# Idle matmuls ahead of the first output tile: float32 zeros in place of bf16 zeros

## The chip, the cores and the metric

The kernel runs on one core of one Trainium2 chip. The metric is the device time of one execution in microseconds, the median of several runs. One more execution was recorded by the hardware profiler; its rows are what the text reads.

## The reference, cut to what matters

A two-step attention (landmarks `p` attend to `k` and `v`; the queries attend to the result) is followed by a feed-forward layer with a quadratic gate:

```python
def _attn_ref(q, k, v, p):                      # 8 batches, 8 heads, 576 tokens, 64 wide, 32 landmarks
    p_packed = sm_attn(p, k, v)
    out = sm_attn(q, p_packed, p_packed)
    return out.astype(np.float32)

def _moe_ref(x, w_in, w_out):                   # x: 4608 x 512, w_in: 512 x 2048, w_out: 2048 x 512
    h = x @ w_in
    g = np.where(h >= 1, h, np.where(h <= -1, 0.0, (h + 1) ** 2 / 4.0))
    return (g @ w_out).astype(np.float32)
```

Nothing of the change takes part in this: the idle matmuls multiply zeros, and what they write is never read.

## The kernel before, in words

For each of the 8 batches the kernel turns `k` and `q` so that the head dimension lies across the partitions (for the first two batches by transposes on TensorE, line 564 and line 601), forms the landmark scores (line 667), exponentiates them (line 676), packs the values with them (lines 735 and 740, "the packed matmul"), and forms the second scores (line 770), their exponentials (line 828) and their sums (line 835). The rows of `w_in` are multiplied with the packed values (line 792, tile `mp`, copied to `M` by line 333), the normalised weights `A` are made by VectorE (line 851), and `M` with `A` gives the hidden tile `h` (line 939). ScalarE and VectorE apply the gate (lines 945 to 960) and leave `hT`; 16 matmuls of 512 columns with `w_out` give an output tile of 128 tokens (line 1030), which is copied and stored. All matmuls take bf16 operands and accumulate in float32.

The order of the work on every engine is written out ahead. `Plan.run` (line 55) simulates the kernel in Python with fixed costs for each step and gives a sorted list; lines 1110 to 1113 emit it in that order, so the program of each engine is fixed, and at run time an instruction waits only for its data and buffers.

The idle matmuls are put in afterwards. Lines 1095 to 1103 walk over the planned steps of TensorE up to the first output matmul and note every planned pause as a number `n` of units: up to 5 us of planned time one unit stands for 0.2135 us, after that for 0.1085 us, with 0.1 us left free. `warm(n)` (line 1105) takes an output tile in PSUM and fills the pause with matmuls of 128 x 128 zeros by 512 columns of zeros, each worth two units, and one of 256 columns where `n` is odd. The operands come from one tile, `zeros` (line 361), which VectorE clears once at the start (line 367). Nobody waits for the idle matmuls, but TensorE works off its instructions in order, so the real matmul behind a burst starts after it.

Of the kernel before, what the change touches and what calls it, by code (L numbers as in the profile page):

```python
# [130 lines left out]
def kernel(  # L131
# [11 lines left out]
    f32 = mybir.dt.float32  # L143
    bf16 = mybir.dt.bfloat16
# [7 lines left out]
    P = 128  # L152
# [9 lines left out]
    FW = 512  # L162
# [150 lines left out]
    const = ctx.enter_context(tc.tile_pool(name="const", bufs=1))  # L313
# [44 lines left out]
    ones2 = const.tile([P, 2, 2], bf16)  # L358
    kz = const.tile([P, H, C5, D], bf16, name="kz")
    vz = const.tile([P, C5, H, D], bf16, name="vz")  # L360
    zeros = const.tile([P, FW], bf16)
    pT_all = const.tile([P, B * Q * G * X * NP + X * NP], bf16, name="pT")
    pT = pT_all[:, :B * Q * G * X * NP].rearrange("p (b a g x n) -> p b a g x n", b=B, a=Q, g=G, x=X)
    hT = const.tile([P, KF, 2 * S], bf16)
# [732 lines left out]
    for t in (t for t in order if t.engine == "PE"):  # L1097
        if t.start >= first_o:
            break
        n = math.ceil((t.start - at) / 0.2135) if at < 5.0 else int((t.start - at - 0.1) / 0.1085)  # L1100
# [3 lines left out]

    def warm(n):
        o = psO.tile([P, d_model], f32, tag="o", name="o")
        for w in [FW] * (n // 2) + [FW // 2] * (n % 2):
            nc.tensor.matmul(o[:, :w], zeros[:, :P], zeros[:, :w], start=True, stop=True)  # L1108

    for t in order:  # L1110
        while fill and t.start > fill[0][0] and t is not consts:
            warm(fill.pop(0)[1])
        t.ways[t.engine][2](t.engine)
# [30 lines left out]
```

## Time and profile before

| | |
|---|---|
| median of 3 runs | 241.79 us (241.51 to 241.95) |
| the profiled execution | 242.18 us |
| its span, first to last instruction | 240.4 us |
| TensorE busy in the span | 233.2 us (97%), 2096 matmuls |
| ScalarE, VectorE, GpSimd busy | 190.0, 179.4 and 37.7 us |
| mean granted clock of TensorE | 0.998 |

In the rows, PE is TensorE's matmul, PEld its weight load, DVE is VectorE, ACT ScalarE, POOL GpSimd; "o<-zeros" names the tile written and the tiles read. Recorded durations of matmuls include the way through the array, so matmuls that follow each other at 0.216 us are shown as lasting 0.379 us each; what a stream of them costs is read from the distance of their starts, or from the chain.

### The profile page before, as it was taken

The page shows a single profiled execution, that of the slowest core. Times are in us where ns is not written, and L with a number is a line of the kernel's source. Part 1 is how long each engine was busy: PE and PEld are TensorE (multiplying, and loading weights), DVE is VectorE, ACT ScalarE, POOL GpSimd, SP SyncE. Part 2 cuts the span into 40 slices and gives each one's busy share as a digit, 9 for nine tenths or more (in the row PEclk, how much of TensorE's full clock was granted, in tenths as well). Part 3 has the DMA queues.
Part 4 walks back from the last instruction along what each step waited for, and adds up shares of the span by engine and source line. Part 5 has one row for each costly group of instructions (what it writes and reads, how often), then busy time and mean ns, then how long its engine had stood idle before and what let it go on. Part 6 is the DMA issues. An engine that isn't in the chain of part 4 may idle for free.

```text
span 240.4 us, 5315 instructions
## 1 busy us (share of the span) xinstructions
PE 233.2 (97%) x2096; PEld 133.9 (56%) x2096; DVE 179.4 (75%) x320; ACT 190.0 (79%) x324; POOL 37.7 (16%) x57
## 2 busy tenths in 40 slices
PE   7799999999999999999999999999999999999993
PEld 3555565565555655466546655656456554654452
DVE  4549997499977996699868989999469967995000
ACT  3578898799989986899889898998789886984211
POOL 8552306000510040070005000300000000000000
PEclk9999999999999999999999999999999999999999
DMA  7999999999999999999999997989301210111315
GB/s 155 201 206 207 203 202 206 199 257 171 148 188 248 186 171 204 187 174 213 204 183 197 218 213 117 138 189 203 97 2 48 74 33 27 44 40 52 98 45 119
DMA packets 65353, 36.42 MB, mean 152 GB/s; under 512 B 34480, under 2 KB 60848, under 8 KB 65328
## 3 DMA queue, kind: packets, MB, share of 16 engines
q0 software_dynamic: 28080, 18.26, 53.5%
q1 hardware_dynamic: 36544, 17.28, 33.4%
q10 hardware_dynamic: 704, 0.56, 0.8%
q8 instruction: 16, 0.26, 0.4%
q14 instruction: 9, 0.07, 0.1%
HBM read 37.22 MB, written 9.44 MB: 194 GB/s over the span
## 4 chain that ended last, share of the span: by engine, by line
PE 92%; ACT 3%; DMA 2%; DVE 1%; issue 0%
PE o L1030 51%; PE h L939 26%; PE mp L792 3%; DMA k_raw<-in_k_dram 2%; PE o L1108 2%; PE pk L730 2%; PE sm L835 2%; PE sp L652 2%; PE s L770 1%; PE tp L564 1%; ACT M L333 1%; PE pk L740 1%; DVE M L333 0%; ACT rc L846 0%; PE tp L601 0%; PE sp L667 0%
## 5 line engine op out<-in xcount | busy, mean ns | idle before, releaser
L1030 PE MATMUL o<-w_out_sb,hT 128*128 128x512 bf16 (+1 forms) x592 | 146.3, 374 | 0.0
L960 DVE SCALAR_TENSOR_TENSOR hT<-t 128x576 bf16<-128x576 f32 (+1 forms) x130 | 91.9, 742 | 3.7 <-ACT t L955 2.1
L945 ACT ACTIVATE x<-h 128x576 f32<-128x576 f32 (+1 forms) x130 | 79.2, 646 | 11.6 <-PE h L939 10.7
L1030 PEld LDWEIGHTS <-hT 128*128 128x128 bf16 x592 | 55.3, 98 | 49.3 <-issue 5.6
L939 PE MATMUL h<-A,M 128*128 128x288 bf16 x512 | 78.1, 286 | 0.6 <-ACT M L333 0.4
L939 PEld LDWEIGHTS <-M 128*128 128x128 bf16 x512 | 49.6, 98 | 27.7 <-issue 1.5
L953 DVE TENSOR_SCALAR t<-x 128x576 f32<-128x576 f32 (+1 forms) x75 | 33.6, 463 | 10.6 <-ACT x L945 10.2
L955 ACT ACTIVATE t<-x 128x576 f32<-128x576 f32 (+1 forms) x55 | 37.0, 684 | 0.9
L333 ACT COPY ob<-o 128x512 f32<-128x512 f32 (+1 forms) x21 | 11.9, 567 | 16.5 <-PE o L1030 16.3
L851 DVE SCALAR_TENSOR_TENSOR A<-eT,rs,rc 128x576 bf16<-128x576 bf16 (+1 forms) x18 | 12.9, 747 | 10.7 <-ACT rc L846 10.7
L333 ACT CAST M<-mp 128x1024 bf16<-128x1024 f32 (+1 forms) x19 | 17.7, 969 | 2.5 <-PE mp L792 2.4
L430 POOL DMA_DIRECT2D v<-in_v_dram x14 | 10.2, 731 | 52.2 <-DVE vz L708 48.9
L430 POOL DMA_DIRECT2D kz<-in_k_dram x14 | 9.7, 701 | 50.9 <-DMA kT<-kz 50.2
L333 DVE CAST M<-mp 128x1024 bf16<-128x1024 f32 (+1 forms) x15 | 17.2, 1147 | 0.4 <-PE mp L792 0.4
L333 DVE COPY ob<-o 128x512 f32<-128x512 f32 x16 | 10.9, 685 | 2.7 <-PE o L1030 2.6
L1108 PE MATMUL o<-zeros 128*128 128x512 bf16 (+1 forms) x42 | 11.4, 405 | 1.2 <-DVE zeros L367 1.2
L828 ACT ACTIVATE eT<-s,rs 128x576 bf16<-128x576 f32 x16 | 11.1, 736 | 1.8 <-PE s L770 1.2
L841 ACT ACTIVATE ln<-sm 128x576 f32<-128x576 f32 x16 | 10.1, 651 | 1.9 <-PE sm L835 1.7
L846 ACT ACTIVATE rc<-ln 128x576 f32<-128x576 f32 (+1 forms) x18 | 10.6, 634 | 0.0
L792 PE MATMUL mp<-w_in_sb,ppT 64*32 64x512 bf16 x256 | 10.3, 380 | 0.0
L674 ACT ACTIVATE ex<-sp 128x640 bf16<-128x640 f32 x14 | 9.5, 702 | 0.3 <-PE sp L652 0.2
L444 POOL DMA_DIRECT2D q<-in_q_dram x11 | 8.4, 762 | 5.1 <-ACT x L945 2.1
(62 smaller groups left out, 110.7 us busy)
## 6 DMA issues: line engine op xcount, KB each, us to landing
out_dram<-ob SPq DMA_DIRECT2D x23, 192.0 KB, 2.7
q<-in_q_dram POOLq DMA_DIRECT2D x7, 576.0 KB, 16.1
out_dram<-ob SPq DMA_DIRECT2D x24, 128.0 KB, 3.9
kz<-in_k_dram POOLq DMA_DIRECT2D x7, 320.0 KB, 6.4
v<-in_v_dram POOLq DMA_DIRECT2D x7, 320.0 KB, 8.6
w_out_sb<-in_moe_w_out_dram POOLq DMA_DIRECT2D x4, 512.0 KB, 15.3
kz<-in_k_dram POOLq DMA_DIRECT2D x7, 256.0 KB, 7.3
v<-in_v_dram POOLq DMA_DIRECT2D x7, 256.0 KB, 9.6
```

Of the source, the lines that this page charges most:

```text
L333: i = (nc.vector.tensor_copy if e == "DVE" else nc.scalar.copy)(to, of)
L430: return G_.dma_start(tokens(nm, b)[p0:p0 + R5, :, :c * D], of)
L792: i = nc.tensor.matmul(have["mp", b, f][a * NP:(a + 1) * NP, g], have["ppT", b][r, g, a], w_in_sb[r, a, f * FW:(f + 1) * FW], start=True, ...
L828: nc.scalar.activation(have["eT", b, g][:, part], have["s2", b, g][:, part, :HALF], AF.Exp, scale=rs_of[b][:, g, 1:])
L851: V.scalar_tensor_tensor(have["A", b][:, g, part], have["eT", b, g][:, part], rs_of[b][:, g, :1], have["rc", b, g][:, part], ALU.mult, ALU ...
L939: nc.tensor.matmul(have["h", b, fi][:, hf, :HALF], have["M", b][:, g, fi * P:(fi + 1) * P], have["A", b][:, g, hf], start=(g == 0), stop=( ...
L945: nc.scalar.activation(have["x", b, fi][:, hs[0]:hs[-1] + 1], have["h", b, fi][:, hs[0]:hs[-1] + 1, :HALF], AF.Prelu, bias=-1.0, alpha=0.5)
L953: V.tensor_scalar(t, x, 1.0, 0.0, ALU.add, ALU.max)
L955: nc.scalar.activation(t, x, AF.Relu, bias=1.0)
L960: V.scalar_tensor_tensor(dst, t, 1.0, t, ALU.min, ALU.mult)
L1030: m = nc.tensor.matmul(have["o", key][:, :w], hT[:, fi, i * P:(i + 1) * P], w_out_sb[:, fi, cols], start=(fi == 0), stop=(fi == KF - 1))
L1108: nc.tensor.matmul(o[:, :w], zeros[:, :P], zeros[:, :w], start=True, stop=True)
```

## The change

The tile of zeros gets half as many elements of twice the width, and `warm` fills a pause with matmuls of 256 float32 columns, one for four units, and one of 64, 128 or 192 columns for a rest of one, two or three units.

```diff
-    zeros = const.tile([P, FW], bf16)
+    zeros = const.tile([P, FW // 2], f32)
...
     def warm(n):
         o = psO.tile([P, d_model], f32, tag="o", name="o")
-        for w in [FW] * (n // 2) + [FW // 2] * (n % 2):
+        for w in [FW // 2] * (n // 4) + [FW // 8 * (n % 4)] * (n % 4 > 0):
             nc.tensor.matmul(o[:, :w], zeros[:, :P], zeros[:, :w], start=True, stop=True)
```

## Rows read from the trace of the kernel before

**Rows 1.** Page: busy us, share, instructions; granted clock in 40 slices.

```profile
PE 233.2 (97%) x2096; PEld 133.9 (56%) x2096; DVE 179.4 (75%) x320; ACT 190.0 (79%) x324; POOL 37.7 (16%) x57
...
PEclk9999999999999999999999999999999999999999
```

**Rows 2.** Page: chain that ended last, shares by engine, by line.

```profile
PE 92%; ACT 3%; DMA 2%; DVE 1%; issue 0%
PE o L1030 51%; PE h L939 26%; PE mp L792 3%; DMA k_raw<-in_k_dram 2%; PE o L1108 2%; PE pk L730 2%; PE sm L835 2%; PE sp L652 2%; PE s L770 1%; PE tp L564 1%; ACT M L333 1%; PE pk L740 1%; DVE M L333 0%; ACT rc L846 0%; PE tp L601 0%; PE sp L667 0%
```

**Rows 3.** Chain in order of time, 0 to 30 us: start, us, what.

```profile
1.23 5.52 DMA k_raw<-in_k_dram
...
7.66 1.11 PE tp L564 x22
8.76 0.11 PE o L1108
...
8.90 1.05 PE sp L667 x24
9.96 1.51 PE o L1108 x7
11.47 0.87 PE pk L735 x48
...
15.89 1.29 PE o L1108 x6
17.18 0.25 PE sm L835 x2
...
17.77 1.94 PE o L1108 x9
19.71 0.49 PE h L939 x4
...
21.16 0.33 PE o L1108 x2
```

**Rows 4.** Timeline, idle matmuls and their loads: start, us, engine, line, what, count.

```profile
1.19 3.22 PE L1108 MATMUL o<-zeros 128*128 128x512 bf16 x8 [1.19 <-DVE zeros L367]
...
4.63 1.36 PE L1108 MATMUL o<-zeros 128*128 128x512 bf16 x6
...
9.75 1.22 PEld L1108 LDWEIGHTS <-zeros 128*128 128x128 bf16 x7
9.79 1.68 PE L1108 MATMUL o<-zeros 128*128 128x512 bf16 x7
...
17.70 2.01 PE L1108 MATMUL o<-zeros 128*128 128x512 bf16 x9
```

**Rows 5.** Timeline, work around the bursts [idle before and its releaser].

```profile
7.16 0.26 PE L564 MATMUL tp<-ident,M 96*128 96x96 bf16 x2 [1.16 <-DVE M L333]
...
9.48 1.50 ACT L676 ACTIVATE ex<-sp 96x768 bf16<-96x768 f32 x2 [0.20 <-PE sp L667]
...
16.23 0.73 ACT L828 ACTIVATE eT<-s,rs 128x576 bf16<-128x576 f32 x1
...
19.02 0.52 DVE L851 SCALAR_TENSOR_TENSOR A<-eT,rs,rc 128x288 bf16<-128x288 bf16 x1
```

**Rows 6.** Line 1108: count, ns min/median/max, first and last start, forms.

```profile
L1108 PEld LDWEIGHTS <-zeros x42: 95/98/152, 1.2 to 21.0; 128*128 128x128 bf16 x42
L1108 PE MATMUL o<-zeros x42: 272/379/634, 1.2 to 21.2; 128*128 128x512 bf16 x36, 128*128 128x256 bf16 x6
```

**Rows 7.** Timeline, weight loads of the first burst.

```profile
1.60 0.15 PEld L1108 LDWEIGHTS <-zeros 128*128 128x128 bf16 x1 [0.28 <-issue]
2.02 0.15 PEld L1108 LDWEIGHTS <-zeros 128*128 128x128 bf16 x1 [0.28 <-issue]
```

**Rows 8.** Timeline, clearing of the zeros tile.

```profile
0.86 0.27 DVE L367 MEMSET zeros<- 128x256 uint32 x1 [0.86 <-PEq L1128]
```

**Rows 9.** Chain by line, 7.66 to 21.49 us.

```profile
by line: PE o L1108 37.5%; PE tp L564 11.1%; PE h L939 8.0%; PE sp L667 7.6%; PE pk L735 6.3%; ACT eT L828 5.3%; PE mp L792 4.9%; PE sm L835 4.7%; DVE ppT L333 4.1%; PE pk L740 2.9%; DVE qT L333 2.3%; issue 2.2%; PE s L770 1.8%; DVE rs L760
```

## The prediction, made before the changed kernel ran

> **What bounds the kernel now.** I began with the page's busy times: TensorE is busy 233.2 of 240.4 us, and the granted clock reads full in every slice [rows 1]. Then the chain that ended last: 92% of it is TensorE, nearly all of that real matmuls of lines 1030 and 939, but 2% is the idle matmuls of line 1108 [rows 2]. So the end is set by TensorE's queue, and the idle matmuls, which compute nothing, have a small share in it. Where they lie is what the chain in order of time shows [rows 3]. Up to 6.75 us the start waits for the load of k_raw; after 7.66 us the chain is on TensorE, and five bursts of idle matmuls stand in it: 0.11 us at 8.76, 1.51 us at 9.96, 1.29 us at 15.89, 1.94 us at 17.77 and 0.33 us at 21.16, together 5.18 us. The two long bursts at 1.19 and 4.63 us [rows 4] are not in it: they run while k_raw is on its way, and the next real matmul, a transpose at 7.16 us, waits for a cast of k_raw [rows 5]. Between them a short transpose of the landmarks stands, whose result nobody needs before the scores at 8.90 us [rows 3]. Two small bursts of 1 and 2 matmuls, among the transposes of q, are not in the chain either. From 21.49 us on there are no idle matmuls, and TensorE hardly rests until its last output tile, so what the five bursts gain or lose reaches the end nearly one for one.
>
> **What the bursts hold.** There are 42 idle matmuls, 36 of 512 columns and 6 of 256 [rows 6]. With the code's unit (256 bf16 columns, planned at 0.1085 us) the lengths give 15, 11, 1, 14, 2, 4, 11, 17 and 3 units, 78 in all; for instance 7 matmuls in the 1.51 us of the chain are 0.216 us each, 0.108 us a unit [rows 3], and the burst at 17.70 us lasts 2.01 us, eight of 512 and one of 256 with the 0.17 us that a matmul shows beyond its distance [rows 4]. In the first burst the loads start 0.42 us apart [rows 7]: 512 columns at 1.2 GHz, though the clock row reads full there. From 4.63 us on five and a half of them take 1.36 us, tail included [rows 4], so the clock is at 2.4 GHz by then, after some 3 us of nothing but idle matmuls.
>
> **The change part by part.**
> The order of all other work is planned in Python from fixed costs, so it does not move; no wait, buffer, or DMA is added. The zeros tile has 1,024 bytes a partition before and after, and its clearing already runs as 256 32-bit elements in 0.27 us [rows 8]: 0.
> Of the bursts, four units become one matmul of 256 float32 columns, and a rest of one to three units becomes one of 64, 128 or 192. That makes 4, 3, 1, 4, 1, 1, 3, 5 and 1 matmuls, 23 in place of 42. The five in the chain are 1, 4, 3, 5 and 1 of these, 14 in place of 25.
> **Array time.** No matmul in this trace takes float32, so this is bounded. From below, 256 float32 columns could cost what 256 bf16 ones do, 0.108 us; by bytes they are 512 bf16 columns, 0.216 us; from above I put 0.43 us (two pairs of 256, that is two matmuls of 512) and two weight loads of 98 ns that nothing hides, 0.63 us. I take 0.43 us, the row of two 512-column matmuls: if the product is built from halves of each operand, every half of one meets every half of the other, and that is four bf16-like passes (an estimate). Then each burst lasts what it lasted: 14 units are 3 x 0.43 + 0.22 = 1.51 us. Difference: 0.
> **Weight loads.** The load of a burst's first weights now shows 0.04 us before its first matmul (9.75 against 9.79 us) and takes 98 ns [rows 4, 6]. With twice the bytes I add another 0.04 us at each of five bursts, 0.2 us. Inside a burst a pass of about 0.2 us hides a load of 98 ns. The rests of 64 columns (after 1 and after 17 units) have 0.11 us of array time in all, too little to hide two loads: 0.05 us each, 0.1 us. The bounds: 0 if all of it is hidden under the matmuls ahead, 2 x 98 ns for each of 14 matmuls, 2.7 us, if nothing is. A gain can come here only from the array time above.
> The Trainium skill ("TensorE: Matmul & The Clock Gate", section "Weight-path perf modes") says that the fast form of the weight load is off for fp32. No row here shows it; by it the loads would stay slow and the sum would move towards the upper end, which is the first rival.
> **The two bursts off the chain** (4 and 3 matmuls) have 1.16 us between the end of the second and the transpose at 7.16 us that waits for the cast [rows 5]; they may grow by a sixth each for nothing.
> **Sum:** 0 + 0.2 + 0.1 = +0.3 us. Against the profiled execution (242.18 us, span 240.4 and 1.78 around it) that is 242.5 us; that execution lies 0.39 us above the median of 241.79 us, so by the median 242.1 us. A change of 0.2%, 0.48 us, is about the least that a measurement of this kernel tells from none, and +0.3 us is under it.
>
> **Rivals.**
> *Weight loads in the open* (slower). If float32 weights can't be loaded beside the running matmul, or TensorE has to run dry between the passes, each of the 14 matmuls on the chain pays one load of 98 ns (+1.4 us, 243.2 us) or two (+2.7 us, 244.5 us). For it: the idle matmuls are the only instructions with another operand type, between bf16 work on both sides. Against it: the bf16 ones hide theirs wholly (42 loads, and 0.216 us from one matmul to the next). It decides from 0.034 us a matmul on (0.48 us over 14).
> *Shorter bursts* (faster). If 256 float32 columns take 0.22 us, TensorE is done early and the next real work starts when its data are there. Each burst is now a bit too long: the second exponential is done at 9.48 + 1.50 = 10.98 us and the packed matmul starts at 11.47 us, some 0.4 us late; the exponential at 16.23 us is done at 16.96 and the sums go on at 17.18 us, 0.2 us; the product A is done at 19.54 us and the hidden matmul goes on at 19.71 us, 0.15 us at most; the last burst perhaps 0.1 us [rows 3, 5]. All of it is 0.85 us, 240.9 us; with half of it, 241.35 us. The clock would survive it: TensorE stood idle for 1.16 us before 7.16 us and its transposes then went 22 in 1.11 us [rows 3, 5], 0.05 us for 96 columns, faster than 1.2 GHz allows.
> The Trainium skill has both sides: "FP8 and Floating Point Precision", section "TensorE Precision Notes", gives true FP32 four passes, by which the sum stands at an array time of 0; "Perfetto Trace Analysis", section "Engine Utilization", halves the output rate for FP32_LOW_HIGH, by which this rival would hold. No row here decides between them.
> *The clock stays low* (slower). The rise to 2.4 GHz came after idle matmuls alone [rows 4, 7], and no row shows float32 ones bring it about. If they don't, the chain's work after 7.66 us runs at 1.2 GHz until real matmuls are dense: up to the packed matmul at 11.47 us that is 3.8 us more (245.6 us), up to 21.49 us TensorE's 85% of 13.8 us, 11.7 us more (253.5 us) [rows 9]. Against it: nothing in the trace ties the clock to the operand's type. It decides if the transposes at 7.16 us still run at 1.2 GHz.
>
> **How the numbers follow.** My forecast, bursts of the same length with slightly dearer entries (241.7 to 242.6 us), has a chance of 0.52; of it 0.42 lies within 0.2%, 0.09 above and 0.01 below. Weight loads in the open: 0.22, all slower. Shorter bursts: 0.14, of it 0.11 faster by over 0.2% and 0.03 within. The clock: 0.12, slower. Sums: faster 0.12, same 0.45, slower 0.43. The range goes from 241.2 us, which leaves out half of the shorter bursts (0.07), to 244.3 us, which leaves out the clock case and the worst of the loads (0.13).
>
> **What would show it.** Right: the burst of 14 units still lasts about 1.5 us, the packed matmul starts at about 11.5 us, the first matmul of line 1030 is 0.2 to 0.4 us later than before, and the transposes from 7.7 us on still go 22 in 1.1 us. Loads in the open: gaps between the idle matmuls, or weight loads of well over 98 ns, and a burst of 14 units of over 1.8 us. Shorter bursts: TensorE idle ahead of the packed matmul and of the sums, with ScalarE named as what it waited for. The clock: transposes 0.08 us apart after 7.66 us, and hidden matmuls of twice the length at 19.7 us. A move that begins only after 21.5 us would make the whole reading wrong.

## The result and the profile after

The changed kernel takes 242.16 us in the median of 14 runs (241.64 to 242.44), the kernel before 241.69 us in runs beside it (241.37 to 241.95). The ratio (of the means) is 1.0016, 95% interval 1.0009 to 1.0023: +0.39 us; the medians lie 0.47 us apart. It is small but clear of no change, though under the 0.48 us (0.2%) that the prediction took for about the least that can be told. Ratios here and below leave out executions more than 1.5% above the fastest of the same kernel. The profiled execution took 242.25 us, span 240.5 us.

The chain that ended last, by engine and by line (page of the changed kernel; against [rows 2]):

```profile
PE 86%; DVE 8%; ACT 3%; issue 2%
PE o L1030 47%; PE h L939 22%; PE o L1108 5%; DVE hT L960 4%; PE mp L792 3%; DVE t L953 2%; PE sm L835 2%; PE sp L652 2%; PE pk L730 1%; PE s L770 1%; PE tp L564 1%; ACT M L333 1%; PE pk L740 1%; DVE M L333 1%; ACT x L945 1%
```

The idle matmuls of line 1108 have 5% of the chain in place of 2%. Most of that is not a longer burst. It is a different start, as the same chain in order of time shows (start, us, what; against [rows 3]):

```profile
1.19 3.56 PE o L1108 x8
...
5.08 2.41 PE o L1108 x6
7.49 1.02 PE tp L564 x24
8.51 0.24 PE o L1108 x2
...
9.70 1.60 PE o L1108 x8
11.30 0.86 PE pk L735 x48
...
15.72 1.39 PE o L1108 x6
...
17.69 2.09 PE o L1108 x10
```

Two things are to be seen. First, the load of k_raw is no longer in the chain: the second burst took 2.41 us where [rows 4] has 1.36, and the transposes waited for it. Second, the bursts on the chain that hold 11 and 17 units last 1.39 and 2.09 us in place of 1.29 and 1.94, the one of 14 units 1.60 in place of 1.51 us, and the small one after the transposes 0.24 in place of 0.11 us.

A chain books a stretch of time under one of two overlapping pieces, so lengths on it need a second look: what the small burst has more, the scores behind it have less (0.96 in place of 1.05 us, though their 24 matmuls take 1.05 us in both timelines). Starts of instructions are safer. From the first matmul of the scores (8.90 us before, [rows 3]) to the first one of line 1030 it is 13.98 us before and 14.31 us here, 0.33 us more. From the first to the last matmul of line 1030 it is 213.50 us before, 213.51 here and 213.49 to 213.51 in every kernel below. So all of the change lies ahead of the first output tile, and it reaches the end one for one. The 8% of VectorE in the chain is another path through the same times. Before (timeline, and line 1030 with its first and last start):

```profile
22.89 0.38 PE L1030 MATMUL o<-w_out_sb,hT 128*128 128x512 bf16 x1
...
L1030 PE MATMUL o<-w_out_sb,hT x592: 272/379/390, 22.9 to 236.4; 128*128 128x512 bf16 x187, 128*128 128x256 bf16 x11
```

and after:

```profile
8.65 1.05 PE L667 MATMUL sp<-pT,kT 128*128 128x64 bf16 x24
...
22.96 0.38 PE L1030 MATMUL o<-w_out_sb,hT 128*128 128x512 bf16 x1
...
L1030 PE MATMUL o<-w_out_sb,hT x558: 272/379/390, 23.0 to 236.5; 128*128 128x512 bf16 x176, 128*128 128x256 bf16 x10
```

The idle matmuls by form (count, ns min/median/max, first and last start; against [rows 6]):

```profile
L1108 PEld LDWEIGHTS o<-zeros x46: 186/190/337, 1.2 to 21.1; 128*128 128x128 f32 x46
L1108 PE MATMUL o<-zeros x46: 219/379/795, 1.2 to 21.2; 128*128 128x256 f32 x30, 128*128 128x192 f32 x8, 128*128 128x64 f32 x4, 128*128 128x128 f32 x4
```

Each of the 23 float32 matmuls runs as two loads and two matmuls, and a load is 190 ns in place of 98. Two passes of 256 float32 columns take as long as two bf16 matmuls of 512, for the bursts last nearly as long as before. So TensorE has not fewer matmuls but a few more: 46 stand where 42 stood.

The first three weight loads of the burst of 17 units in the timeline of the changed kernel

```profile
17.62 0.30 PEld L1108 LDWEIGHTS o<-zeros 128*128 128x128 f32 x2 [0.23 <-issue]
17.95 0.19 PEld L1108 LDWEIGHTS o<-zeros 128*128 128x128 f32 x1
```

and in that of the kernel before:

```profile
17.70 0.11 PEld L1108 LDWEIGHTS <-zeros 128*128 128x128 bf16 x2 [0.23 <-issue]
17.93 0.10 PEld L1108 LDWEIGHTS <-zeros 128*128 128x128 bf16 x1
```

The third load stands 0.33 us behind the first, with bf16 0.23 us; from there on both follow at about 0.21 us. The first load of a float32 burst has no matmul of its burst over it, and the burst begins about 0.10 us later for it. Which of the two, the longer load or the other operand type, costs that time is what the experiments have to tell apart.

### The profile page after: what moved, and what is told of

Read it like the earlier page. It is cut to its first block, busy times and chain, and to the rows that moved or that the text cites. A ratio compares the mean times of both kernels' runs of the same rounds, so it can differ in the third digit from the quotient of the medians.

```text
span 240.5 us, 5289 instructions
## 1 busy us (share of the span) xinstructions
PE 232.2 (97%) x2066; PEld 139.7 (58%) x2100; DVE 179.8 (75%) x320; ACT 190.1 (79%) x324; POOL 37.6 (16%) x57
## 4 chain that ended last, share of the span: by engine, by line
PE 86%; DVE 8%; ACT 3%; issue 2%
PE o L1030 47%; PE h L939 22%; PE o L1108 5%; DVE hT L960 4%; PE mp L792 3%; DVE t L953 2%; PE sm L835 2%; PE sp L652 2%; PE pk L730 1%; PE s L770 1%; PE tp L564 1%; ACT M L333 1%; PE pk L740 1%; DVE M L333 1%; ACT x L945 1%
## 5 line engine op out<-in xcount | busy, mean ns | idle before, releaser
L1030 PE MATMUL o<-w_out_sb,hT 128*128 128x512 bf16 (+1 forms) x558 | 139.7, 373 | 2.2 <-issue 0.9
L945 ACT ACTIVATE x<-h 128x576 f32<-128x576 f32 (+1 forms) x130 | 79.3, 646 | 11.8 <-PE h L939 10.9
L1108 PE MATMUL o<-zeros 128*128 128x256 f32 (+3 forms) x46 | 13.4, 434 | 1.2 <-DVE zeros L367 1.2
L1108 PEld LDWEIGHTS o<-zeros 128*128 128x128 f32 x46 | 9.9, 232 | 3.0 <-DVE zeros L367 1.2
```

The lines of the kernel that those rows point to most:

```text
L945: nc.scalar.activation(have["x", b, fi][:, hs[0]:hs[-1] + 1], have["h", b, fi][:, hs[0]:hs[-1] + 1, :HALF], AF.Prelu, bias=-1.0, alpha=0.5)
L1030: m = nc.tensor.matmul(have["o", key][:, :w], hT[:, fi, i * P:(i + 1) * P], w_out_sb[:, fi, cols], start=(fi == 0), stop=(fi == KF - 1))
```

## The experiments

The theory after this reading: float32 costs at the entry of the bursts on the chain. The rival: the first two bursts make the difference, where TensorE's clock rises late, from 1.2 to 2.4 GHz. (The trace's own clock record puts the rise at 4.11 us in the profile before and at 7.11 us in the profile after. The column of the granted clock reads 1.00 ahead of the first recorded rise, so there the level has to be read from the distance of the matmuls.)

**The changed kernel once more.**

> The changed kernel once more, beside the kernel before. Theory (float32 bursts cost an entry on the chain): 0.3 to 0.5 us above the kernel before, and the bursts of 14, 11 and 17 units again last 1.60, 1.39 and 2.09 us on the chain, against 1.51, 1.29 and 1.94 us, whatever the clock does ahead of them. Rival (it is the first two bursts, which run longer where TensorE's clock rises late, 7.11 us in the first profile against 4.11 us before): where the rise comes by 4.5 us, the time is that of the kernel before within 0.2 us.

Ratio 1.0013 (1.0002 to 1.0024), +0.3 us. Its chain in order of time:

```profile
1.23 4.80 DMA k_raw<-in_k_dram
...
6.94 1.11 PE tp L564 x22
...
10.84 0.87 PE pk L735 x48
...
15.27 1.39 PE o L1108 x6
...
17.23 2.09 PE o L1108 x10
```

The same program, and in this execution the clock rose early (at 4.17 us; second burst 1.46 us), k_raw is back in the chain, and the bursts on the chain are as long as in the first profile. Their length does not hang on the start. From the first of 22 transposes to the packed matmul it is 3.90 us, before 3.81: 0.09 us more; from the scores to the first output matmul it is 14.31 us again. Its span is 240.0 us, 0.5 us under that of the first profile, and its hidden matmuls start 0.46 us sooner. So the start moves single executions by as much as the whole change does, and only medians of many runs tell the change. This one execution took 241.79 us, which is the median of the kernel before: as a time it would suit the rival as well, and what speaks against the rival is the length of the bursts.

**Float32 in the first two bursts alone, and in the other seven alone.** Both tiles of zeros are there (VectorE clears one more, in 0.27 us at 1.1 us), and a burst takes one or the other by its planned time:

```diff
...
+        four = at < 6.0          # the second kernel: at >= 6.0
+        z = zeros4 if four else zeros
+        for w in ([FW // 2] * (n // 4) + [FW // 8 * (n % 4)] * (n % 4 > 0) if four else [FW] * (n // 2) + [FW // 2] * (n % 2)):
+            nc.tensor.matmul(o[:, :w], z[:, :P], z[:, :w], start=True, stop=True)
```

> Float32 zeros in the first two bursts alone, bf16 in the seven behind. Theory (the cost is paid by the bursts on the chain after 8.5 us): 0 to 0.1 us above the kernel before, bursts of 14, 11 and 17 units at 1.51, 1.29 and 1.94 us. Rival (the first two bursts): the whole of the change's 0.4 us, with the first burst 0.3 us longer than the 3.22 us of before.

> bf16 zeros in the first two bursts, float32 in the seven behind. Theory: 0.3 to 0.45 us above the kernel before, the bursts of 14, 11 and 17 units at 1.60, 1.39 and 2.09 us. Rival: within 0.1 us of the kernel before in time.

First two: ratio 0.9997 (0.9985 to 1.0008). Other seven: 1.0009 (1.0000 to 1.0017), +0.2 us, with 0 and 0.4 us as its ends. The chains decide more sharply than the times. Float32 in the first two:

```profile
7.52 1.02 PE tp L566 x24
...
11.24 0.87 PE pk L737 x48
...
15.67 1.29 PE o L1112 x6
```

Float32 in the other seven:

```profile
4.90 2.16 PE o L1112 x6
7.06 1.02 PE tp L566 x24
...
10.88 0.87 PE pk L737 x48
...
15.30 1.39 PE o L1112 x6
...
17.27 2.09 PE o L1112 x10
```

With the same 24 transposes, the way to the packed matmul is 3.72 us with bf16 bursts and 3.82 us with float32 ones; the burst of 11 units 1.29 and 1.39 us, that of 17 units 1.94 and 2.09 us. The theory holds in the chains; the times of the two kernels, whose intervals are 0.4 and 0.6 us wide, would not decide alone. The starts in the timelines give it stretch by stretch (us, from the first matmul of one to the first matmul of the next; the column "holds" has the idle bursts between them):

| stretch | holds | before | first two | changed | again | other seven | bf16 first | rest of one in bf16 |
|---|---|---|---|---|---|---|---|---|
| scores to packed matmul | 14 units | 2.49 | 2.49 | 2.58 | 2.58 | 2.58 | 2.49 | 2.58 |
| packed matmul to projection (line 792) | 2, 4 and 11 units | 5.96 | 5.97 | 6.06 | 6.05 | 6.06 | 6.02 | 6.06 |
| projection to hidden matmuls (line 939) | 17 units | 2.19 | 2.19 | 2.34 | 2.34 | 2.34 | 2.19 | 2.28 |
| hidden matmuls to first output matmul | 3 units | 3.34 | 3.34 | 3.34 | 3.34 | 3.33 | 3.34 | 3.34 |
| all four | | 13.98 | 13.98 | 14.31 | 14.31 | 14.30 | 14.04 | 14.25 |

The last two columns are the next two experiments. The change costs 0.09 us in the first stretch, 0.09 to 0.10 in the second and 0.15 in the third, 0.33 us in all; it does so whether the first two bursts are float32 or not. The burst of 1 unit costs nothing: with the transposes done in one go, the scores start 1.33 us behind the first of them both with bf16 (first two, bf16 first) and with float32 (changed, other seven).

The second kernel also answers another question. Its second burst is bf16 and still takes 2.16 us: the late rise of the clock (here at 6.63 us) comes with bf16 zeros too, as the early one at 4.17 us came with float32 ones. The first kernel's first burst is 3.57 us long, as the rival said, where the bf16 one takes 3.38 us in a profile whose clock also rises late. In that profile the transposes wait for the second burst, so it may cost something in such executions; the time shows no cost (0.9997, at most 0.2 us by its interval).

**bf16 for the first two units of each burst, float32 behind them.**

```diff
...
+        early = min(n, 2)
+        for z, w in ([(zeros, FW // 2 * early)] + [(zeros4, FW // 2)] * ((n - early) // 4)
+                     + [(zeros4, FW // 8 * ((n - early) % 4))] * ((n - early) % 4 > 0)):
+            nc.tensor.matmul(o[:, :w], z[:, :P], z[:, :w], start=True, stop=True)
```

> Every burst begins with bf16 zeros for its first two units (a burst of one or two units is bf16 alone), float32 behind them. If the entry costs because a float32 weight load of 0.19 us is not hidden under the short matmuls ahead of the burst, it is now hidden under a bf16 matmul of 0.216 us, and the kernel is within 0.15 us of the one before. If it costs because TensorE changes the operand type, the change is still made in six bursts and the time stays 0.3 us or more above. Rival (the first two bursts in whatever form): 0.3 us or more above as well, but with bursts of 1.51, 1.29 and 1.94 us on the chain.

Ratio 0.9999 (0.9987 to 1.0011): within 0.3 us of the kernel before. The chain and the table tell more:

```profile
7.50 1.02 PE tp L566 x24
...
11.22 0.87 PE pk L737 x48
...
15.65 1.35 PE o L1112 x7
...
17.59 0.16 issue
17.75 1.78 PE o L1112 x8
```

The stretch to the packed matmul is 3.72 us again and the burst of 17 units 0.16 + 1.78 = 1.94 us (the record of its first matmul is missing, and its time stands as "issue"); only the burst of 11 keeps 0.06 of 0.10 us. That burst now ends on a float32 rest of one unit (2 + 8 + 1 units), which it does not have in the changed kernel, and 0.06 us is what such a rest costs in the next experiment too. From the scores to the first output matmul it is 14.04 us, with 14.31 in the changed kernel and 13.98 before. The change of operand type is still made in every burst longer than two units, and costs nothing that the chain shows. What costs is a float32 load with nothing over it that is long enough.

**A rest of one unit in bf16.**

```diff
...
+        for z, w in ([(zeros4, FW // 2)] * (n // 4) + [(zeros4, FW // 8 * (n % 4))] * (n % 4 > 1)
+                     + [(zeros, FW // 2)] * (n % 4 == 1)):
```

> The changed kernel, but a rest of one unit (the burst of 1 unit and the last of the burst of 17) is a bf16 matmul of 256 columns in place of 64 float32 columns. Theory (the chain pays 0.10 us where a float32 load opens a burst and 0.05 us more where two loads stand over only 0.11 us of array time): the stretch from the turned k to the packed matmul is back to the length of the kernel before (the burst of 1 unit is bf16 again), the bursts of 11 and 17 units keep 0.10 us each; in all 0.2 us above the kernel before in place of 0.35. Rival (each burst of float32 costs the same 0.1 us, whatever its rest): the burst of 17 units stays at 2.09 us and the stretch to the packed matmul is 0.1 us longer, 0.35 us in all.

Ratio 1.0011 (1.0002 to 1.0020), +0.3 us, closer to what the rival expects; the time doesn't tell 0.2 from 0.35. The chain:

```profile
8.27 1.05 PE sp L669 x24
9.32 1.60 PE o L1111 x8
10.92 0.87 PE pk L737 x48
...
15.35 1.39 PE o L1111 x6
...
17.32 2.03 PE o L1111 x9
```

Half of it came as expected: the burst of 17 units falls from 2.09 to 2.03 us, so the 64-column rest cost 0.06 us there, and 0.09 of its 0.15 us is the entry. The other half is a miss. The way from the scores to the packed matmul is as long as in the changed kernel (2.58 us by the starts, 2.49 before): the theory had put these 0.10 us down to the burst of 1 unit, and they belong to the entry of the 14 units. In all it is 14.25 us to the first output matmul, 0.27 us above the kernel before.

**Every unit a float32 matmul of its own.**

```diff
-        for w in [FW // 2] * (n // 4) + [FW // 8 * (n % 4)] * (n % 4 > 0):
+        for w in [FW // 8] * n:
```

> The changed kernel with every unit of a pause a float32 matmul of its own, 64 columns each: the same columns in all, 78 matmuls with two weight loads each in place of 23. It measures the float32 load by itself. Theory (a load of 0.19 us is hidden only while a pass of about 0.2 us runs): two loads set the pace, some 0.2 us a unit in place of 0.108, bursts of 14, 11 and 17 units last 2.8, 2.2 and 3.4 us on the chain, 3 to 4 us more in all, 245 to 246 us. Rival (loads overlap with whatever runs, and the cost at the entry has another cause): bursts stay within 0.2 us of 1.6, 1.4 and 2.1 us and the time within 0.5 us of the changed kernel.

Median 267.49 us (4 runs: 254.47, 267.45, 267.52 and 268.99; the one of 267.45 is profiled, and no trace shows what was otherwise in the one of 254.47): both expectations far off, and for a reason neither had. First the loads of line 1108, then two pieces of the chain:

```profile
L1108 PEld LDWEIGHTS o<-zeros x156: 190/333/337, 1.2 to 46.5; 128*128 128x128 f32 x156
```

```profile
13.06 1.92 PE tp L564 x24
...
16.77 6.03 PE o L1108 x28
```

28 passes of 64 columns take 6.03 us, 0.215 us each. A pass of 256 columns takes 0.213 us at 2.4 GHz, so the array time of 64 is about 0.11 us at 1.2 GHz (an estimate from that), half of what they take: the load sets the pace, as the theory said. And the 24 transposes of 96 columns take 1.92 us, 0.08 us each, which is 1.2 GHz. The clock had not risen by 13 us, and it did not rise for long after, as the hidden matmuls in the timeline show:

```profile
45.30 0.95 PE L939 MATMUL h<-A,M 128*128 128x288 bf16 x4
46.08 0.78 PE L1108 MATMUL o<-zeros 128*128 128x64 f32 x6
46.70 1.63 PE L939 MATMUL h<-A,M 128*128 128x288 bf16 x12
```

Four take 0.95 us at 45.3 us, twelve take 1.63 us at 46.7 us. The clock record has the rise at 45.91 us. From 1.2 to 45 us TensorE's matmuls were busy without a break (43.80 of 43.80 us), and its weight loads for 40.70 us of that; which of the two kept the clock low no run tells. Behind the rise the float32 passes follow at 0.11 us, 0.22 us a unit: the 0.2 us that the theory put would have come out at the higher clock. The rival "the clock stays low" of the prediction is thus real, only not for the bursts that the change makes.

**Shorter bursts, bf16.** Three kernels cut the bursts that were a bit too long for their pauses:

```diff
+    fill[1] = (fill[1][0], 4)                                                       # the second burst: 11 to 4 units
...
+    fill = fill[:2]                                                                 # none behind the second
...
+    fill = [(at, n) for (at, _), n in zip(fill, (15, 4, 0, 10, 2, 2, 8, 14, 0)) if n]  # all cut
```

> The kernel before with its second burst cut from 11 units to 4, bf16 as before. In the profiles where TensorE's clock rose late (6.6 to 7.3 us) the second burst ran at 1.2 GHz for 2.2 to 2.5 us and ended after the casts of k_raw, so that the transposes waited for it. Theory: this holds in most runs, and the kernel gets 0.2 to 0.4 us faster than the one before, its transposes start with the casts. Rival (the casts end last in most runs, and late rises are the exception): within 0.1 us of the kernel before.

> The kernel before without the seven bursts behind the second one. Theory (each burst on the chain is a little longer than its pause, and the clock outlives pauses of up to 2 us): 0.4 to 0.9 us faster than the kernel before, transposes and hidden matmuls as long as before. Rival (the clock falls back to 1.2 GHz somewhere before 24 us): slower by 1 us or more, with hidden matmuls 0.24 us apart at about 20 us in place of 0.12.

> The kernel before with every burst cut to what its pause needs by the times at which the data are there: 15, 4, 0, 10, 2, 2, 8, 14 and 0 units in place of 15, 11, 1, 14, 2, 4, 11, 17 and 3. Theory: 0.5 to 1.0 us faster than the kernel before, the packed matmul starts 0.3 to 0.4 us sooner behind the scores. Rival (what is saved ahead of the first output tile is lost again behind it, to ScalarE and VectorE): less than 0.2 us faster though the hidden matmuls start 0.5 us sooner.

All three are slower: ratios 1.0046 (1.0027 to 1.0065), 1.0065 (1.0052 to 1.0078) and 1.0035 (1.0022 to 1.0047). (A fifth execution of the last took 481.42 us, with nothing on record that says why.) The clock is what they lost. Stretches of the kernel with the short second burst (window and its length; busy us of PE, PEld, DVE, ACT and POOL with their instructions; granted clock; DMA share and GB/s):

```profile
8.00:10.00 2.00, 1.75 (x29) 1.48 (x28) 1.73 (x3) 1.54 (x4) 0.42 (x1) 0.60 1.31 201
10.00:12.00 2.00, 2.00 (x6) 0.68 (x5) 0.87 (x3) 0.58 (x1) 1.47 (x2) 0.55 1.31 199
12.00:14.00 2.00, 2.00 (x74) 1.72 (x73) 0.38 (x2) 0.39 (x2) 1.95 (x4) 1.00 1.26 205
```

of the one without later bursts:

```profile
14.00:18.00 4.00, 2.29 (x20) 0.63 (x19) 1.30 (x4) 3.21 (x7) 1.63 (x3) 0.50 1.24 206
18.00:24.00 6.00, 5.30 (x28) 2.65 (x29) 5.02 (x13) 4.27 (x11) 1.47 (x3) 0.51 1.24 206
```

and of the one with all cut:

```profile
8.00:10.00 2.00, 1.86 (x35) 1.71 (x33) 1.73 (x3) 1.46 (x3) 0.57 (x1) 0.60 1.31 201
```

Behind a second burst of 4 units TensorE stood idle for 1.07 us before the transposes, and the clock was at 1.2 GHz from about 8.4 to 11.8 us. The idle time alone does not decide it: in the profile of the kernel before it was 1.16 us there [rows 5], and the clock stayed. Nor was it lost in every execution: two of the twelve runs of this kernel took 241.37 and 241.63 us, no more than the kernel before. In the kernel without later bursts the clock fell at 13.6 us and rose again at 23.8 us, and until it fell no pause of TensorE behind the first burst was longer than 0.89 us: the 2 us that the theory trusted it with are not borne out. Before the fall the times are as expected: its packed matmul starts 1.94 us behind the scores, in place of 2.49. The late rise as the usual case, which the first of the three was to test, could not be tested so.

**A little shorter, bf16.**

```diff
+    fill = [(at, n) for (at, _), n in zip(fill, (15, 11, 1, 12, 2, 4, 10, 16, 3))]
```

> The kernel before with three bursts on the chain slightly cut, bf16: 12, 10 and 16 units in place of 14, 11 and 17; the first two bursts as before. The earlier cuts lost the clock behind a second burst of 4 units, or without any burst behind the second. Theory (the clock is safe with both first bursts whole and nearly all of the later ones): 0.3 to 0.45 us faster than the kernel before, no dip of the granted clock before 24 us. Rival (the pauses are needed in full): the clock dips to 1.2 GHz before 24 us and the kernel is slower than the one before; or the data are late where the bursts end, and nothing is gained.

Median 241.46 us against 241.69, ratio 0.9988 (0.9979 to 0.9997): 0.3 us faster than the kernel before, and so faster than both. The granted clock reads 1.00 in every stretch from 4 to 24 us. The chain has the burst of 12 units at 1.29 us, 0.22 less, and the scores to the packed matmul at 2.35 in place of 2.57 us. Behind it something is given back (timeline, projection of the packed values):

```profile
16.50 0.10 PEld L792 LDWEIGHTS <-ppT 64*32 64x32 bf16 x5 [0.24 <-issue]
16.50 0.79 PE L792 MATMUL mp<-w_in_sb,ppT 64*32 64x512 bf16 x8
...
16.90 0.10 PEld L792 LDWEIGHTS <-ppT 64*32 64x32 bf16 x3 [0.30 <-issue]
```

Eight matmuls take 0.79 us in place of 0.41, with a stop before the second four. Those read the second half of the first part of w_in, which comes as a load of its own. The fifth matmul waits for that load's semaphore, whose last update by the DMA comes at 16.86 us, and starts at 16.90; in the kernel before the last update comes at 16.79 us and the projection starts at 17.36. So this profile shows no gain: it starts early (scores at 8.27 us), and from the scores to the first output matmul it takes 14.14 us, 0.16 us more than before. The 0.3 us of the median come from other executions than the profiled one (241.70 us, the second slowest of eleven). That they start later, so that the load is there in time, is argued, not shown.

## Why the prediction was right

The forecast was +0.3 us, and +0.39 us came (0.2 to 0.55 by the interval); the traces have 0.33 us between the scores and the first output matmul, and nothing behind it. The mechanism was the one forecast, bursts of the same array time with a dearer entry; that the sum fits so well is partly luck, since its terms were off in both directions. Of the signs that were named, the first matmul of line 1030 comes 0.33 us later behind the scores; counted from the start of the span it is only 0.07 us later (22.96 and 22.89 us), because the scores started 0.25 us earlier in that execution. Point by point:

- **Array time, 0:** right in time. The trace has two passes per float32 matmul, each as long as a bf16 matmul of 512 columns (0.21 us for 256), where the prediction spoke of four like those of bf16; it comes to the same 0.43 us. With the entries taken off (bf16 ahead), the bursts of 14 and 17 units last as long as before. By this the Trainium skill ("FP8 and Floating Point Precision", section "TensorE Precision Notes", four passes for true FP32) agrees with the trace in the array time of 256 columns, and the halved rate of "Perfetto Trace Analysis", section "Engine Utilization", does not describe the whole matmul: it fits one of the two passes.
- **Weight loads, 0.2 + 0.1:** the right sum from wrong terms. The entry was put at 0.04 us for each of five bursts; it is 0.09 to 0.10 us for three of them (14, 11 and 17 units) and nothing for the other two: the stretch with the burst of 3 units is 3.34 us with either type, and the scores start no later behind a float32 burst of 1 unit. The rests of 64 columns were put at 0.05 us each; the one behind 16 units costs 0.06, the other nothing. 3 x 0.09 + 0.06 is 0.33 us. The load was put at 98 ns and a little more; it is 190 ns.
- **The first two bursts, nothing:** right in the sum, and wrong in its reason. They were said to run under the load of k_raw with 1.16 us to spare. That held in the profile before, whose k_raw came late (its casts ended at 7.6 us) and whose clock rose early. In the first profile after, and in the five others of kernels with both bursts whole whose clock rose later than 6 us (the first two, the other seven, bf16 first, the rest of one in bf16, and the one without later bursts; the kernel of single units is left out), the transposes waited for the second burst instead. Two of these have bf16 in both bursts, and the time of the kernel with float32 in these two alone shows no cost (at most 0.2 us by its interval); but the spare time was a property of one execution.
- **Loads in the open:** not at this size: inside a burst a pass of 0.21 us covers a load. With passes of 64 columns the loads do set the pace.
- **Shorter bursts:** the premise was wrong, and so was its price. "The clock would survive it" was argued from one idle stretch of 1.16 us; with bursts cut to their data the clock fell. A cut of 4 units in 42 (14, 11 and 17) gives 0.3 us in the median; the larger cuts tried gave a loss.
- **The clock stays low:** not here; the early rise at the repeat (4.17 us) and the late rise with bf16 zeros (6.63 us) show that the operand type of these bursts alone does not decide it. Whether it shifts the odds is not measured.

## What to carry to other kernels

An idle matmul in front of real work is not free filling: here the first weight load of a burst stood on the chain, and a short last pass with two loads cost too, so the form with the shortest load at the edges of a burst was the best, and a wider operand in the middle changed nothing. A pause that holds the clock should be cut in small steps with the granted clock of each stretch beside it. Where two things race at the start (a load and a burst under a clock that rises at another moment each time), one profile shows one winner, and what has to spare in it may have none in the next.

## What was not expected of the hardware

- A float32 matmul shows as two loads and two matmuls; a load of 128 float32 columns took 190 ns at 2.4 GHz against 98 ns. Under short passes such loads set a pace of 0.215 us at 1.2 GHz and 0.11 us at 2.4 GHz.
- TensorE can be busy without a break and stay at 1.2 GHz: it did from 1.2 to 45.9 us where every pause was filled with float32 passes of 64 columns between loads, and that execution took 26 us more than the kernel before.
- The rise to 2.4 GHz came at times between 4.1 and 7.3 us in executions of kernels whose first burst has the same 15 units, bf16 or float32, in matmuls of up to 512 or 256 columns.
